# A planner's rule on VectorE and GpSimd: two-operand operations no longer exclude GpSimd

## The chip, the cores and the metric

The kernel runs on one core of a Trainium2 chip. Its engines work side by side, each through its own list of instructions in order: TensorE (PE in the profile; PEld is its weight load) multiplies, VectorE (DVE) and ScalarE (ACT) do elementwise work and reductions, GpSimd (POOL) does elementwise work on SBUF alone, and SyncE (SP) issues DMAs. The metric is device time in microseconds (us) for one execution, lower is better.

## The reference

Sliding-window attention with sink tokens, followed by a feed-forward network whose weights are float64 values drawn as float32; int64 and float64 inputs arrive as pairs of 32-bit words.

```python
# q, k, v: (4, 8, 768, 64) float32; n_sink = 4, window = 128
scores = matmul(q, k.transpose) / 8
keep   = (key < n_sink) | (0 <= query - key < window)
a      = exp(where(keep, scores, -1e9) - rowmax)
a      = a / (a.sum(-1) + 1e-9)
x      = matmul(a, v), heads merged        # (3072, 512)

h  = x @ w_in                              # (3072, 2048)
sp = log1p(exp(min(h, 20)))                # h itself above 20
y  = (h * tanh(sp)) @ w_out                # (3072, 512)
```

## The kernel before

The 3072 tokens are cut into 12 chunks of 256 (2 blocks of 128 queries). The four chunks that begin a batch come first, since their attention is smaller (plain fp32 products); the other eight follow. For each chunk there is attention in four pairs of heads (`pair`), then 8 steps of the feed-forward network (`step`), each over two 128-wide slices of the hidden dimension, `f`. The weights stay in SBUF. The first three chunks (`GROUP`) are taken in turn, two steps each (`PART`), so that the weights can be unpacked while they run; from chunk 3 on a chunk runs through its 8 steps alone, and all of these but the last chunk's have a form of their own (`wide`). Chunks are numbered from 0 in the order in which they run.

**Split values.** Products that need more precision than one fast pass are done in parts: a value m becomes a rounded copy gh and a rest gl = m - gh. So a rounded copy (`copy_ways`, lines 256 on ACT, 258 and 259 on VectorE) is followed nearly everywhere by a subtraction (`sub_ways`, line 267 on GpSimd, line 269 on VectorE). There are four kinds of subtraction: `gl<-n,gh` (hidden values, 96 of them, the last two given to VectorE alone), `w<-w,w` (32 rests of weights and 32 of Q), `w<-raw,w` (64 of K, on 64 partitions) and `w<-att,w` (48 rests of x, which read PSUM and are given to VectorE alone).

**Weights** (`weights`, 32 times): a DMA brings a 128x512 tile of float64 bit patterns (`raw`); s1 scales the high words (L297 on ACT, L298 on VectorE), s2 shifts (L300), s3 puts the sign in (L301), s4 masks the exponent (L303), s5 scales the low words (L305), s6 adds both (the join: L308 on GpSimd, L309 on VectorE), s7 copies and s8 subtracts.

**A step**: two groups of products into `hp` (L493 and L494 in wide steps, L497 in the others); in wide steps a reduction adds hp's two halves into n (L503). Then exp (L506, ACT), min (L507, VectorE), square, log, exp (L508, L509, L510, ACT), and one VectorE operation on u and h (L511), where h is n in SBUF for wide steps and hp in PSUM for the others. Then the copy to gh and the subtraction to gl, and the second products into `acc` (L527), those with gh first, those with gl behind.

**Attention of a pair**: Q K products (L396, or L399 from chunk 4 on), masked minimum (L407, VectorE, from PSUM), exp (L410, ACT), the normaliser (L413 or L414, L415), scaling by it (L420 on VectorE or L421 on ACT), transposes on PE (L431, L440), copies to SBUF, and the products with V (L449, L453).

**The plan.** All this is written as tasks with a rank, a few `ways` (engine, duration in ns, the call) and what they depend on. `Plan.solve` is a list scheduler that runs when the program is built: of all tasks that are ready it takes the one with the earliest start (plus the way's penalty, the fourth entry), and among equal starts the lowest rank. The order that comes out is kept on every engine, so on the chip each engine works through it however late things run. A scalar `port` stands for what VectorE and GpSimd share: a task on GpSimd, or one whose way has a fifth entry, starts only when `port` is free and holds it to its end. `shared()` makes such a way:

```python
def shared(way, pen=0):
    return way[0], way[1], 0, pen, True
...
ports = lambda t, e: e == POOL or len(t.ways[e]) > 4
...
key = (max(r, free[e]) + (t.ways[e][3] if len(t.ways[e]) > 3 else 0), rank[id(t)])
```

[...]

**Ranks.** `att_rank` places a pair's attention a number of steps ahead of the chunk that uses it: 20, 14 and 8 for the first three, and from chunk 3 on `min(LEAD, LEADN + (n - GROUP) / 2)`, with `LEADN` = 9. A pair's K, Q and V loads rank 3 steps (V 2) ahead of that; the splitting of K and Q follows 1.5 steps behind the loads. `OTP` places the transposes within the pair, and `OVP` the products with V.

Of the kernel before, what the change touches and what calls it, by code (L numbers as in the profile page):

```python
# [16 lines left out]
U32 = mybir.dt.uint32  # L17
AF = mybir.ActivationFunctionType
ALU = mybir.AluOpType
# [17 lines left out]
SIGN = -2147483648  # L37
# [3 lines left out]
PE, ACT, DVE, POOL, SP = "pe", "act", "dve", "pool", "sp"  # L41
# [1 line left out]
LAG = {PE: {PE: 0, ACT: 200, DVE: 200}, ACT: {PE: 270, ACT: 143, DVE: 142, POOL: 170}, DVE: {PE: 200, ACT: 120, DVE: 127, POOL: 155},  # L43
       POOL: {PE: 203, ACT: 75, DVE: 80, POOL: 102}, SP: {}}
W2 = 2 * P + SK
PEN_C, PEN_S, PEN_N, PEN_J = 200, 0, 0, 0
OTP, OVP = 1.2, 1
WA, WB, WO = 1.5, -5, 1.5
GROUP, PART = 3, 2
LEAD, LEADG, LEADN = 11, (20, 14, 8), 9  # L50
WARM, SPARE, ROOM = 14, 250, 4
ZERO = 224
SPL = 1.5
# [5 lines left out]
def f32(ap):  # L59
    return ap.bitcast(F32)  # L60


def act_t(n, psum=False, ptr=0):
    return (n + (61 if psum else 112)) / 1.2 + 93 * ptr


def dve_t(n, fast=False):
    return ((n / 2 if fast else n) + 66) / 0.96


def shared(way, pen=0):

    return way[0], way[1], 0, pen, True


def pool_t(n):
    return 149 + 2.1 * n


def pe_t(*ns):  # L80
# [25 lines left out]
class Plan:  # L106
# [6 lines left out]
    def add(self, prio, ways, deps=(), bufs=(), new=()):  # L113
        deps = {id(d): d for d in list(deps) + [b.maker for b in bufs] if d is not None}
        t = Task(prio, ways, list(deps.values()), list(bufs) + list(new), list(new))
        for b in t.bufs:
            b.users += 1
        for b in new:
            b.maker = t
        self.tasks.append(t)  # L120
        return t
# [108 lines left out]
class Fast(Base):  # L230
# [32 lines left out]
    def sub_ways(self, n, dst, a, b, engines=(POOL, DVE)):  # L263
        nc = self.nc
        ways = {}
        if POOL in engines:
            ways[POOL] = pool_t(n), lambda: nc.gpsimd.tensor_tensor(dst(), a(), b(), ALU.subtract)  # L267
        if DVE in engines:
            way = dve_t(n), lambda: nc.vector.tensor_tensor(dst(), a(), b(), ALU.subtract)  # L269
            ways[DVE] = shared(way, PEN_S) if POOL in engines else way  # L270
        return ways

    def load(self, prio, buf, dst, src, kb, **kw):
# [12 lines left out]
    def weights(self, f, rank):  # L286
        nc, add = self.nc, self.plan.add
        deps = []
        for src, nm in ((self.w_in, "wi"), (self.w_out, "wo")):
            raw = Buf("raw", [P, 512, 2], I32)  # L290
            z, e, hi, lo = Buf("w", [P, 512], I32), Buf("w", [P, 512], I32), Buf("w", [P, 512], F32R), Buf("w", [P, 512], F32R)
            hi.users, lo.users = 1, 1
            z.brief = e.brief = True
            r = rank if nm == "wi" else rank + WO
            ld = self.load(r - 1.0, raw, lambda raw=raw: raw.t.rearrange("p n t -> p (n t)"), src[f].bitcast(I32), 512)
            hw = lambda raw=raw: raw.t[:, :, 1]
            s1 = add(r, {ACT: (act_t(512), lambda z=z, hw=hw: nc.scalar.activation(f32(z.t), f32(hw()), AF.Copy, scale=2.0 ** -112)),  # L297
                         DVE: shared((dve_t(512), lambda z=z, hw=hw: nc.vector.tensor_scalar(f32(z.t), f32(hw()), 2.0 ** -112, None, ALU.mult)), PEN_C)},  # L298
                     [ld], [raw], [z])
            s2 = add(r + .01, {DVE: shared((dve_t(512, True), lambda z=z: nc.vector.tensor_scalar(z.t, z.t, 3, None, ALU.logical_shift_left)))}, [s1], [z])  # L300
            s3 = add(r + .02, {DVE: shared((dve_t(512), lambda z=z, hw=hw: nc.vector.scalar_tensor_tensor(  # L301
                z.t, hw(), SIGN, z.t, ALU.bitwise_and, ALU.bitwise_or)))}, [s2], [raw, z])
            s4 = add(r + .03, {DVE: shared((dve_t(512, True), lambda z=z, e=e: nc.vector.tensor_scalar(  # L303
                e.t, z.t, EXPM, None, ALU.bitwise_and)))}, [s3], [z], [e])
            s5 = add(r + .04, {DVE: shared((dve_t(512), lambda raw=raw, e=e: nc.vector.scalar_tensor_tensor(  # L305
                f32(e.t), raw.t[:, :, 0].bitcast(U32), 2.0 ** -52, f32(e.t), ALU.mult, ALU.mult)))}, [s4], [raw, e])
            s6 = add(r + .06, {
                POOL: (pool_t(512), lambda z=z, e=e: nc.gpsimd.tensor_tensor(f32(z.t), f32(z.t), f32(e.t), ALU.add)),  # L308
                DVE: shared((dve_t(512), lambda z=z, e=e: nc.vector.tensor_tensor(f32(z.t), f32(z.t), f32(e.t), ALU.add)), PEN_J)}, [s5, s3], [z, e])  # L309
            s7 = add(r + .07, self.copy_ways(512, lambda hi=hi: hi.t, lambda z=z: f32(z.t)), [s6], [z], [hi])  # L310
            s8 = add(r + .08, self.sub_ways(512, lambda lo=lo: lo.t, lambda z=z: f32(z.t), lambda hi=hi: f32(hi.t)), [s7], [z, hi], [lo])
            self.wh[nm].append(hi)
            self.wl[nm].append(lo)
            deps += [s7, s8]
        return deps
# [152 lines left out]
    def step(self, st, f2, rank, begins, ends, wdeps, last, wide):  # L468


        nc, add = self.nc, self.plan.add
# [4 lines left out]
        r = rank - (SH if last else 0)  # L476
        eager = last and f2 >= NF // 2 - QUICK
        u, m = Buf("u", [P, 2, T]), Buf("n", [P, 2, T])
# [26 lines left out]
        h = m if wide else hp  # L505
        a = add(r + .5, {ACT: (act_t(N, not wide), lambda: nc.scalar.activation(u.t, h.t, AF.Exp))}, hs or g1, [h], [u])  # L506
        a = add(r + .51, {DVE: shared((dve_t(N, True), lambda: nc.vector.tensor_scalar(u.t, u.t, E20, None, ALU.min)))}, [a], [u])  # L507
        a = add(r + .52, {ACT: (act_t(N, ptr=1), lambda: nc.scalar.activation(u.t, u.t, AF.Square, bias=self.one))}, [a], [u])  # L508
        a = add(r + .53, {ACT: (act_t(N, ptr=1), lambda: nc.scalar.activation(u.t, u.t, AF.Ln, bias=self.half, scale=0.5))}, [a], [u])  # L509
        a = add(r + .54, {ACT: (act_t(N), lambda: nc.scalar.activation(u.t, u.t, AF.Exp, scale=-1.0))}, [a], [u])  # L510
        way = dve_t(N), lambda: nc.vector.scalar_tensor_tensor(m.t, u.t, 1.0, h.t, ALU.subtract, ALU.mult)  # L511
        e = add(r + .55, {DVE: shared(way) if wide else way}, [a], [u, h], [] if wide else [m])
        gg = add(r + .57, self.copy_ways(N, lambda: gh.t, lambda: m.t), [e], [m], [gh])
        gk = add(r + .58, self.sub_ways(N, lambda: gl.t, lambda: m.t, lambda: f32(gh.t)), [gg], [m, gh], [gl])
        if eager:
# [2 lines left out]
        r = rank  # L518
# [380 lines left out]
```

## Time and profile before

| | |
|---|---|
| time, median of 2 runs | 735.19 us (734.97 to 735.41) |
| the profiled execution, its own time | 734.82 us |
| its span, first to last instruction | 732.8 us |
| granted TensorE clock, mean | 0.998 |
| GpSimd: subtractions and joins | 101, of 254 that may run there |
| `gl<-n,gh` on GpSimd / on VectorE | 32, mean 1293 ns / 64, mean 754 ns |
| `w<-w,w` (L267 / L269) | 24, mean 1387 ns / 40, mean 727 ns |
| `w<-raw,w` on GpSimd / on VectorE | 24, mean 1214 ns / 40, mean 658 ns |
| joins L308 / L309 | 21, mean 1403 ns / 11, mean 688 ns |

Busy time is the union of an engine's records, and its share is an average over the whole span, so it has to be read by stretches. A group's line reads: code line, engine, operation, what is written from what, shape and count, then busy us and the mean ns of one, then the engine's idle time ahead of it and what ended that. [...]

### The profile page before, as it was taken

The page shows a single profiled execution, that of the slowest core. Times are in us where ns is not written, and L with a number is a line of the kernel's source. Part 1 is how long each engine was busy: PE and PEld are TensorE (multiplying, and loading weights), DVE is VectorE, ACT ScalarE, POOL GpSimd, SP SyncE. Part 2 cuts the span into 40 slices and gives each one's busy share as a digit, 9 for nine tenths or more (in the row PEclk, how much of TensorE's full clock was granted, in tenths as well). Part 3 has the DMA queues.
Part 4 walks back from the last instruction along what each step waited for, and adds up shares of the span by engine and source line. Part 5 has one row for each costly group of instructions (what it writes and reads, how often), then busy time and mean ns, then how long its engine had stood idle before and what let it go on. Part 6 is the DMA issues. An engine that isn't in the chain of part 4 may idle for free.

```text
span 732.8 us, 12975 instructions
## 1 busy us (share of the span) xinstructions
PE 717.3 (98%) x4468; PEld 605.3 (83%) x4468; DVE 543.9 (74%) x1419; ACT 569.8 (78%) x1288; POOL 134.0 (18%) x109
## 2 busy tenths in 40 slices
PE   6999999999999999999999999999999999999996
PEld 4667889888888888888888888888888888888995
DVE  5999999996778877768877667777777867664432
ACT  5999989777977788787788878787787788775653
POOL 0232231201120222121012121130132223100000
PEclk9999999999999999999999999999999999999999
DMA  6555433423353323323233323223313311100000
GB/s 212 163 172 166 139 103 133 124 86 90 103 138 93 82 75 89 81 74 98 65 92 93 79 65 102 72 64 111 87 45 95 109 31 34 49 17 2 30 1 33
DMA packets 48987, 64.12 MB, mean 87 GB/s; under 512 B 4880, under 2 KB 41744, under 8 KB 48912
## 3 DMA queue, kind: packets, MB, share of 16 engines
q1 hardware_dynamic: 48480, 61.62, 29.0%
q10 hardware_dynamic: 432, 1.57, 0.6%
q8 instruction: 37, 0.61, 0.4%
q14 instruction: 38, 0.31, 0.1%
HBM read 56.89 MB, written 6.29 MB: 86 GB/s over the span
## 4 chain that ended last, share of the span: by engine, by line
PE 90%; DVE 4%; ACT 4%; DMA 1%; issue 1%; SPq 0%; ACTq 0%; DVEq 0%
PE acc L527 35%; PE hp L493 16%; PE hp L497 10%; PE hp L494 8%; PE att L449 5%; PE att L399 4%; PE att L431 4%; PE att L453 3%; PE att L497 2%; ACT p L410 1%; PE att L396 1%; DMA qh<-q_p 1%; ACT p L421 1%; DVE p L407 1%; ACT w L256 1%; DVE w L305 1%
## 5 line engine op out<-in xcount | busy, mean ns | idle before, releaser
L527 PE MATMUL acc<-w,gh 128*128 128x512 f32 x768 | 198.4, 396 | 0.2 <-ACT gh L256 0.2
L493 PE MATMUL hp<-w,w 128*128 128x512 f32 x512 | 192.1, 409 | 0.0
L527 PEld LDWEIGHTS acc<-w,gh 128*128 128x128 f32 x768 | 136.1, 188 | 26.3 <-ACT gh L256 0.8
L494 PE MATMUL hp<-w,w 128*128 128x256 f32 x512 | 143.3, 280 | 0.0
L503 DVE TENSOR_REDUCE n<-hp 128x256 f32<-128x512 f32 x128 | 87.8, 687 | 30.5 <-PE hp L494 29.6
L493 PEld LDWEIGHTS hp<-w,w 128*128 128x128 f32 x512 | 96.3, 188 | 17.1 <-issue 0.2
L527 PE MATMUL acc<-w,gl 128*128 128x512 f32 x384 | 108.3, 390 | 0.0
L410 ACT ACTIVATE p<-p,nm 128x288 f32<-128x288 f32 (+1 forms) x192 | 95.3, 499 | 3.6 <-DVE nm L407 3.5
L494 PEld LDWEIGHTS hp<-w,w 128*128 128x128 f32 x512 | 96.8, 189 | 1.5
L407 DVE CUSTOM_DVE_ANT_0 p<-att,m 128x288 f32<-128x288 f32 (+1 forms) x192 | 74.6, 419 | 25.2 <-PE att L399 20.2
L508 ACT ACTIVATE u<-u,bias 128x512 f32<-128x512 f32 x96 | 69.0, 720 | 29.8 <-DVE u L507 29.8
L497 PE MATMUL hp<-w,w 128*128 128x256 f32 x672 | 89.6, 285 | 0.2 <-DVE n L511 0.2
L497 PEld LDWEIGHTS hp<-w,w 128*128 128x128 f32 x672 | 84.9, 191 | 3.9 <-issue 0.5
L527 PEld LDWEIGHTS acc<-w,gl 128*128 128x128 f32 x384 | 71.9, 188 | 14.1
L506 ACT ACTIVATE u<-n 128x512 f32<-128x512 f32 x64 | 40.5, 632 | 54.1 <-DVE n L503 54.1
L267 POOL TENSOR_TENSOR gl<-n,gh 128x512 fp32r<-128x512 f32 x32 | 41.4, 1293 | 202.6 <-ACT gh L256 173.1
L256 ACT ACTIVATE gh<-n 128x512 fp32r<-128x512 f32 x93 | 58.3, 626 | 20.4 <-DVE n L511 20.3
L507 DVE TENSOR_SCALAR u<-u 128x512 f32<-128x512 f32 x96 | 44.7, 466 | 38.2 <-ACT u L506 37.6
L509 ACT ACTIVATE u<-u,bias 128x512 f32<-128x512 f32 x96 | 68.9, 718 | 1.7
L511 DVE SCALAR_TENSOR_TENSOR n<-u,n 128x512 f32<-128x512 f32 x64 | 44.1, 690 | 35.1 <-ACT u L510 34.9
L510 ACT ACTIVATE u<-u 128x512 f32<-128x512 f32 x96 | 60.1, 627 | 1.8
L269 DVE TENSOR_TENSOR gl<-n,gh 128x512 fp32r<-128x512 f32 x64 | 48.2, 754 | 15.4 <-PE acc L527 12.2
(85 smaller groups left out, 1063.3 us busy)
## 6 DMA issues: line engine op xcount, KB each, us to landing
raw<-k_p SPq DMA_DIRECT2D x64, 224.0 KB, 3.5
w<-q_p SPq DMA_DIRECT2D x64, 128.0 KB, 3.2
raw<-w_out SPq DMA_DIRECT2D x15, 512.0 KB, 4.0
raw<-w_in SPq DMA_DIRECT2D x14, 512.0 KB, 3.5
y<-u SPq DMA_DIRECT2D x24, 256.0 KB, 2.0
vt<-v_b SPq DMA_DIRECT2D x32, 192.0 KB, 2.5
vsr<-v_s SPq DMA_DIRECT2D x32, 128.0 KB, 2.3
ks<-k_p SPq DMA_DIRECT2D x16, 144.0 KB, 3.4
```

The costliest lines, as they stand in the source:

```text
L256: ways[ACT] = act_t(n, psum), lambda: nc.scalar.activation(dst(), src(), AF.Copy, scale=scale or 1.0)
L269: way = dve_t(n), lambda: nc.vector.tensor_tensor(dst(), a(), b(), ALU.subtract)
L407: a = add(r + .03 + .01 * e, {DVE: (dve_t(n) + 8, lambda st=st, pv=pv, nm=nm, e=e, mask=mask, n=n: nc.vector.tensor_tensor_reduce(out=pv() ...
L410: a = add(r + .05 + .01 * e, {ACT: (act_t(n, ptr=2), lambda pv=pv, nm=nm, sm=sm, e=e: nc.scalar.activation(pv(), pv(), AF.Exp, bias=nm.t[: ...
L493: yield nc.tensor.matmul(hp.t, wih[f].t[:, fs], xt, start=kt == 0, stop=False)
L494: yield nc.tensor.matmul(hp.t[:, 0, :], wil[f].t[:, fs], xt[:, 0, :], start=False, stop=kt == KT - 1)
L497: yield nc.tensor.matmul(hp.t[:, y, :], w_.t[:, fs], xt[:, z, :], start=kt == 0 and n_ == 0, stop=kt == KT - 1 and n_ == 2)
L503: hs.append(add(r + .3 + .1 * y, {DVE: (dve_t(2 * T), lambda y=y, hp=hp: nc.vector.tensor_reduce(m.t[:, y, :], hp.t.rearrange("p z t -> p ...
L508: a = add(r + .52, {ACT: (act_t(N, ptr=1), lambda: nc.scalar.activation(u.t, u.t, AF.Square, bias=self.one))}, [a], [u])
L509: a = add(r + .53, {ACT: (act_t(N, ptr=1), lambda: nc.scalar.activation(u.t, u.t, AF.Ln, bias=self.half, scale=0.5))}, [a], [u])
L510: a = add(r + .54, {ACT: (act_t(N), lambda: nc.scalar.activation(u.t, u.t, AF.Exp, scale=-1.0))}, [a], [u])
L527: yield nc.tensor.matmul(acc[t].t, g_.t[:, y, ts_], w_.t, start=new and n_ == 0, stop=done)
```

## The change

In the plan, `shared()` is taken off the VectorE ways that read two operands: the subtractions of `sub_ways`, s3, s5 and s6 of the weights, and L511 in wide steps. It also goes from s1 on VectorE, which reads one operand with a stride. The one-operand operations s2, s4, L507, L420 and the SBUF copies keep it. Penalties change: 150 ns on a subtraction on VectorE where GpSimd could take it (0 before), 250 on the join (0 before), 100 on copies on VectorE (200 before). GpSimd's duration in the plan goes from 149 + 2.1 n to 200 + 2.15 n ns. `OTP` goes from 1.2 to 1.0 and `LEAD` from 11 to 9. The instructions themselves, their operands and number stay; which of two engines does an operation, and the order on every engine, come from the plan.

```diff
-PEN_C, PEN_S, PEN_N, PEN_J = 200, 0, 0, 0
-OTP, OVP = 1.2, 1
+PEN_C, PEN_S, PEN_N, PEN_J = 100, 150, 0, 250
+OTP, OVP = 1.0, 1.0
...
-LEAD, LEADG, LEADN = 11, (20, 14, 8), 9
+LEAD, LEADG, LEADN = 9, (20, 14, 8), 9
...
 def pool_t(n):
-    return 149 + 2.1 * n
+    return 200 + 2.15 * n
...
     def sub_ways(self, n, dst, a, b, engines=(POOL, DVE)):
...
             way = dve_t(n), lambda: nc.vector.tensor_tensor(dst(), a(), b(), ALU.subtract)
-            ways[DVE] = shared(way, PEN_S) if POOL in engines else way
+            ways[DVE] = (*way, 0, PEN_S) if POOL in engines else way
...
             s1 = add(r, {ACT: (act_t(512), lambda z=z, hw=hw: nc.scalar.activation(f32(z.t), f32(hw()), AF.Copy, scale=2.0 ** -112)),
-                         DVE: shared((dve_t(512), lambda z=z, hw=hw: nc.vector.tensor_scalar(f32(z.t), f32(hw()), 2.0 ** -112, None, ALU.mult)), PEN_C)},
+                         DVE: (dve_t(512), lambda z=z, hw=hw: nc.vector.tensor_scalar(f32(z.t), f32(hw()), 2.0 ** -112, None, ALU.mult), 0, PEN_C)},
...
-            s3 = add(r + .02, {DVE: shared((dve_t(512), lambda z=z, hw=hw: nc.vector.scalar_tensor_tensor(
-                z.t, hw(), SIGN, z.t, ALU.bitwise_and, ALU.bitwise_or)))}, [s2], [raw, z])
+            s3 = add(r + .02, {DVE: (dve_t(512), lambda z=z, hw=hw: nc.vector.scalar_tensor_tensor(
+                z.t, hw(), SIGN, z.t, ALU.bitwise_and, ALU.bitwise_or))}, [s2], [raw, z])
...
-            s5 = add(r + .04, {DVE: shared((dve_t(512), lambda raw=raw, e=e: nc.vector.scalar_tensor_tensor(
-                f32(e.t), raw.t[:, :, 0].bitcast(U32), 2.0 ** -52, f32(e.t), ALU.mult, ALU.mult)))}, [s4], [raw, e])
+            s5 = add(r + .04, {DVE: (dve_t(512), lambda raw=raw, e=e: nc.vector.scalar_tensor_tensor(
+                f32(e.t), raw.t[:, :, 0].bitcast(U32), 2.0 ** -52, f32(e.t), ALU.mult, ALU.mult))}, [s4], [raw, e])
             s6 = add(r + .06, {
                 POOL: (pool_t(512), lambda z=z, e=e: nc.gpsimd.tensor_tensor(f32(z.t), f32(z.t), f32(e.t), ALU.add)),
-                DVE: shared((dve_t(512), lambda z=z, e=e: nc.vector.tensor_tensor(f32(z.t), f32(z.t), f32(e.t), ALU.add)), PEN_J)}, [s5, s3], [z, e])
+                DVE: (dve_t(512), lambda z=z, e=e: nc.vector.tensor_tensor(f32(z.t), f32(z.t), f32(e.t), ALU.add), 0, PEN_J)}, [s5, s3], [z, e])
...
         way = dve_t(N), lambda: nc.vector.scalar_tensor_tensor(m.t, u.t, 1.0, h.t, ALU.subtract, ALU.mult)
-        e = add(r + .55, {DVE: shared(way) if wide else way}, [a], [u, h], [] if wide else [m])
+        e = add(r + .55, {DVE: way}, [a], [u, h], [] if wide else [m])
```

## What was predicted

> **What bounds the kernel now.** I read the page from the top: its first row for busy shares, its slices for where they hold.
>
> ```profile
> span 732.8 us, 12975 instructions
> PE 717.3 (98%) x4468; PEld 605.3 (83%) x4468; DVE 543.9 (74%) x1419; ACT 569.8 (78%) x1288; POOL 134.0 (18%) x109
> PE   6999999999999999999999999999999999999996
> DVE  5999999996778877768877667777777867664432
> ```
>
> TensorE (PE) is busy in every slice but the first and last, but VectorE (DVE) is full too in the first quarter. So the kernel has two stages. Busy time by stretch (PE, PEld, DVE, ACT, POOL; then clock and DMA) says the same, and shows that the granted clock is full:
>
> ```profile
> 25.00:50.00 25.00, 23.45 (x181) 15.76 (x181) 24.65 (x98) 24.14 (x86) 8.21 (x6) 1.00 0.62 188
> 50.00:100.00 50.00, 49.42 (x345) 40.69 (x344) 48.80 (x133) 48.80 (x120) 12.02 (x9) 1.00 0.43 133
> 100.00:150.00 50.00, 50.00 (x324) 45.09 (x323) 49.61 (x105) 42.87 (x86) 11.47 (x8) 1.00 0.39 128
> 150.00:200.00 50.00, 50.00 (x330) 44.30 (x329) 38.73 (x84) 39.19 (x78) 6.09 (x5) 1.00 0.33 91
> 400.00:500.00 100.00, 100.00 (x604) 84.60 (x603) 71.28 (x181) 79.87 (x179) 21.21 (x17) 1.00 0.29 79
> ```
>
> PE's busy time includes filler: matmuls on zeros that the plan puts where it foresees idle time (line 622). The same view for that line alone (PE, PEld):
>
> ```profile
> 25.00:100.00 75.00, 9.22 (x68) 6.13 (x68) 1.00 0.49 152
> 100.00:733.00 633.00, 0.35 (x2) 0.20 (x2) 1.00 0.27 76
> ```
>
> Between 25 and 100 us PE stands idle for 1.55 + 0.58 us and multiplies zeros for 9.22: 11.3 us. That is all a better plan can win there; after 100 us only 0.35 us of filler is left and PE has no gap. VectorE and ScalarE set the pace up to 100 us, PE after it. The stretch ahead of 25 us has filler too, but it waits for first loads and holds few subtractions; I take nothing from it.
>
> **The change, part by part.** The first part lets the plan run VectorE's operations on two operands beside GpSimd (POOL). Whether the chip does so is seen where the two met by accident. Around 100 us the timeline shows (start, duration), VectorE first:
>
> ```profile
> 99.32 0.69 DVE L305 SCALAR_TENSOR_TENSOR w<-raw,w 128x512 f32<-128x512 uint32 x1
> 99.92 0.68 DVE L309 TENSOR_TENSOR w<-w,w 128x512 f32<-128x512 f32 x1
> 100.53 0.68 DVE L511 SCALAR_TENSOR_TENSOR n<-u,hp 128x512 f32<-128x512 f32 x1
> 101.91 1.68 DVE L269 TENSOR_TENSOR gl<-n,gh 128x512 fp32r<-128x512 f32 x1
> ...
> 100.09 1.68 POOL L308 TENSOR_TENSOR w<-w,w 128x512 f32<-128x512 f32 x1 [7.00 <-DVE w L305]
> 101.74 1.30 POOL L267 TENSOR_TENSOR w<-w,w 128x512 fp32r<-128x512 f32 x1
> ```
>
> The subtraction at 101.91 met a GpSimd subtraction already running until 103.04; it took 1.68 us and ended 0.55 after it. Its kind takes 0.69, so 0.99 was spent standing still. The other way round, GpSimd's addition at 100.09 began inside L309 and took 1.68 instead of 1.30. The exception is L511 at 100.53, inside that addition: 0.68, undisturbed. Its second operand, hp, lies in PSUM. So the exclusion holds for two operands in SBUF, which is what the old plan assumes. The new plan drops a true constraint. Also read off here: VectorE's records overlap by 0.08 (starts at 99.32, 99.92, 100.53), so such an operation costs its engine 0.605 us.
>
> [...]
>
> Stage one, 25 to 150 us. Groups of that window (count, busy, mean ns):
>
> ```profile
> L305 DVE SCALAR_TENSOR_TENSOR w<-raw,w 128x512 f32<-128x512 uint32 x26 | 18.0, 705 | 0.1
> L301 DVE SCALAR_TENSOR_TENSOR w<-raw,w 128x512 int32<-128x512 int32 x26 | 17.6, 686 | 0.0
> L269 DVE TENSOR_TENSOR w<-w,w 128x512 fp32r<-128x512 f32 x22 | 15.2, 699 | 0.1
> L269 DVE TENSOR_TENSOR gl<-n,gh 128x512 fp32r<-128x512 f32 x14 | 12.6, 896 | 0.0
> L309 DVE TENSOR_TENSOR w<-w,w 128x512 f32<-128x512 f32 x7 | 4.8, 687 | 0.0
> L300 DVE TENSOR_SCALAR w<-w 128x512 int32<-128x512 int32 x26 | 10.8, 421 | 0.0
> L303 DVE TENSOR_SCALAR w<-w 128x512 int32<-128x512 int32 x26 | 10.7, 422 | 0.0
> L507 DVE TENSOR_SCALAR u<-u 128x512 f32<-128x512 f32 x15 | 6.3, 422 | 0.0
> L420 DVE TENSOR_SCALAR p<-p,rc 128x128 f32<-128x128 f32 (+1 forms) x15 | 6.2, 417 | 0.1
> ...
> L308 POOL TENSOR_TENSOR w<-w,w 128x512 f32<-128x512 f32 x19 | 26.5, 1399 | 87.2 <-DVE w L305 79.9 <-DVE rc L415 7.4
> L267 POOL TENSOR_TENSOR w<-w,w 128x512 fp32r<-128x512 f32 x4 | 5.3, 1332 | 6.2 <-ACT w L256 6.1
> ```
>
> What must run one at a time: 95 operations on two SBUF operands (26 + 26 + 22 + 14 + 7) at 0.605 = 57.5 us; 82 on one operand at 0.42 less the overlap of 0.08 = 27.9; 23 of GpSimd's at 1.30 = 29.9. Sum 115 of 125 us: the shared resource is 92% full already.
>
> What can move is the 43 subtractions and additions still on VectorE (22 + 14 + 7). GpSimd holds 23 of 66; I read "most" as three quarters, 50, so 27 move (guess between 10 and 43). VectorE gets 27 x 0.605 = 16.3 us back, GpSimd takes 27 x 1.30 = 35.1. Demand on the shared resource becomes 115 + 18.8 = 134 us in 125: 9 us too many. With 10 moved it is 122 and fits; with all 43 it is 145, 20 too many. It is full at 14 moves (10 us over 0.695). So VectorE's relief can't be had: an operation of 0.605 leaves it, and the next one that needs the port stands behind 1.30 of GpSimd. How much of the 9 us is on PE's path? From 150 to 200 us VectorE is idle for 11.3 us and can take work that slips; against that, PE follows the order of a plan that does not know the delay. I take half: **+4.5**. Ends: -11.3 (all filler and gaps go) and +20.
>
> Cruise, 200 to 650 us. In 400 to 500 (counts as above):
>
> ```profile
> L511 DVE SCALAR_TENSOR_TENSOR n<-u,n 128x512 f32<-128x512 f32 x14 | 9.7, 690 | 3.4 <-ACT u L510 3.4
> L269 DVE TENSOR_TENSOR gl<-n,gh 128x512 fp32r<-128x512 f32 x10 | 7.2, 722 | 0.0
> L269 DVE TENSOR_TENSOR w<-raw,w 64x448 fp32r<-64x448 f32 x5 | 3.1, 623 | 0.2
> L269 DVE TENSOR_TENSOR w<-w,w 128x512 fp32r<-128x512 f32 x2 | 1.4, 686 | 0.0
> ```
>
> These are 17 subtractions on VectorE beside 17 on GpSimd (21.21 us in the stretch, above). Three quarters of 34 is 25 or 26, so 8.5 move and GpSimd is busy for 21.2 + 8.5 x 1.25 = 32 us in 100. VectorE has 29 us idle here, so its relief buys nothing: PE is the bound. What can hurt is L511, two SBUF operands, in the chain from hp to gh that feeds PE. In the old plan it was kept clear of GpSimd. Now one in three of the 14 meets a GpSimd operation and waits half of it: 4.5 waits of 0.63. What covers them is the time between the copy of gh (ACT) and the weight load that needs it:
>
> ```profile
> 397.87 0.62 ACT L256 ACTIVATE gh<-n 128x512 fp32r<-128x512 f32 x1
> 398.59 1.72 PEld L527 LDWEIGHTS acc<-w,gh 128*128 128x128 f32 x8
> ...
> 418.11 0.62 ACT L256 ACTIVATE gh<-n 128x512 fp32r<-128x512 f32 x1
> 421.07 1.68 PEld L527 LDWEIGHTS acc<-w,gh 128*128 128x128 f32 x8
> ```
>
> The cover is 0.10 us in one step and 2.34 in another. If half the steps are tight, 2.25 waits lose 0.4 each: 0.9 us in 100, times 4.5 = **+4**. Ends: 0 (all covered) and 4.5 x 0.63 x 4.5 = +13. After 650 us little is left to move.
>
> The penalties and GpSimd's dearer price (1301 ns for 512 columns in the plan, against the 1300 at 101.74) only steer which engine is picked; the moves above contain them. Copies freer to use VectorE: this concerns SBUF copies and PSUM copies, where ACT has 20 us idle in 100 and VectorE 29. Neither bounds the cruise: 0, and if VectorE were full as in stage one, a cast there costs 0.34 us of the full resource, ten of them 3.4 (in the upper end). Transposes 0.2 step earlier, and attention of chunks 4 to 11 led by 9 steps instead of 9.5 to 11: these change ranks, not work. The chain of waits gives the step:
>
> ```profile
> 398.88 2.76 PE acc L527 x12
> 458.04 2.79 PE acc L527 x12
> ```
>
> 59.2 us for a chunk of 8 steps, 7.4 us a step; so transposes move 1.5 us forward and the last five chunks' attention up to 14.8 us back, with its K, Q and V loads on SP's queue. The slowest of those lands in 3.5 us and is issued 1.5 steps, 11 us, ahead of its first use:
>
> ```profile
> raw<-k_p SPq DMA_DIRECT2D x64, 224.0 KB, 3.5
> ```
>
> Chunk 3 has a lead of 9 already and its stretch shows no filler. I take 0, ends -1.5 and +3.
>
> **Sum.** The profiled execution took 734.8 us in all (span 732.8); the median is 0.4 above it. 734.8 + 4.5 + 4 = 743.3, plus 0.4: **744 us**.
>
> **The rivals.** *Relief wins (faster).* In stage one VectorE is 98% busy; if a moved subtraction blocks it for less than the 0.605 us that it frees, filler shrinks. Place: 25 to 100 us; price: about 7 of the 11.3 us, 728. It decides when VectorE's next operations are mostly on PSUM (L407, L511 with hp), which a GpSimd operation did not slow. Against it: 85 of VectorE's 125 us there are port work. *Nothing comes of it, 735.* GpSimd still keeps clear of one-operand work, so the plan finds few openings and moves under 14, or the cover of up to 2.34 us swallows the waits. For it: the old plan's collisions above cost PE nothing visible. *The port runs over, on the path (slower).* Nearly all 43 move, two thirds of the 20 us land on PE, and the cruise loses 8: 734.8 + 13 + 8 = 756. For it: from 100 us on PE has no filler, so lost time isn't made up.
>
> **How the numbers follow.** A small loss (738 to 749.5) 0.50; relief 0.16; nothing 0.14; overrun 0.20. The predicted time is the likeliest case's. The range 731 to 757 leaves out most of relief (0.11) and the upper part of the overrun (0.08). Two per cent, about what a measurement tells from no change, is 14.7 us: faster than 720.5 would need more than all filler and gaps of stage one, 0.02; slower than 749.9 is the overrun, 0.20; the rest 0.78.
>
> **What would show it.** Right: GpSimd's count over 150 and its busy share near 35%; in 25 to 150 us L301, L305, L309 and L269 with means well over 690 ns; GpSimd's L267 at 1.4 and more; idle time or longer gaps on PE between 25 and 200 us; L511 on n in the cruise over 690. Wrong: those means unchanged while GpSimd is fuller (the exclusion isn't what the rows suggest); less filler and an earlier end of the third chunk (relief); GpSimd's count near 109 (nothing moved). A slower cruise with L511 unchanged would put the loss on the ranks instead.

## The result, and the profile after

The changed kernel takes 769.32 us (median of 2 runs, 768.82 to 769.81) against 735.19: a ratio of 1.0466 with a 95% interval of 1.0449 to 1.0484, so 34 us slower. The prediction was 744 with a range to 757: the sign was right, and the loss was four times as large. The profiled execution took 769.81 us, with this page:

```profile
span 768.0 us, 13016 instructions
PE 728.8 (95%) x4432; PEld 603.7 (79%) x4432; DVE 561.7 (73%) x1342; ACT 562.9 (73%) x1262; POOL 272.4 (35%) x212
PE   6898998788999999999999999999999999999997
DVE  5999989998678668677677677678678667865322
```

GpSimd's busy share is 35%, as forecast. VectorE's total went up (543.9 to 561.7 us) although it runs 77 instructions fewer: the first sign that its instructions became longer. TensorE has lost slices in the first quarter, which the stretches show in us (PE, PEld, DVE, ACT, POOL, then clock and DMA):

```profile
25.00:50.00 25.00, 21.53 (x155) 14.25 (x155) 24.88 (x91) 21.39 (x71) 10.99 (x8) 1.00 0.59 165
50.00:100.00 50.00, 44.08 (x277) 35.30 (x274) 46.55 (x107) 37.87 (x96) 27.86 (x20) 0.91 0.40 119
100.00:150.00 50.00, 44.05 (x271) 37.15 (x269) 47.92 (x85) 35.65 (x70) 26.43 (x18) 0.98 0.34 111
150.00:200.00 50.00, 43.87 (x266) 37.84 (x267) 42.51 (x64) 33.03 (x58) 26.27 (x19) 1.00 0.29 82
400.00:500.00 100.00, 98.68 (x585) 82.20 (x584) 72.12 (x174) 74.98 (x168) 33.46 (x26) 1.00 0.29 82
```

From 50 to 200 us TensorE now stands idle for 18 us (150 less 44.08, 44.05 and 43.87), where it had half a microsecond. VectorE is as busy from 25 to 200 us as before: the DVE column adds up to 161.9 us, and to 161.8 in the rows of before, with GpSimd at 92 us instead of 38. The work that left VectorE was replaced by standing still. The clock column is new too: 0.91 and 0.98, where the same stretches of before had 1.00.

How much of the 34 us belongs to which stage can be read from one line of each trace, the reductions that only the wide steps (chunks 3 to 10) have. Before, then after, in the view of the tile n; "209.7 to 679.0" are the starts of the first and the last of them:

```profile
L503 DVE TENSOR_REDUCE n<-hp x128: 670/686/693, 209.7 to 679.0; 128x256 f32<-128x512 f32 x128
```

```profile
L503 DVE TENSOR_REDUCE n<-hp x128: 669/683/693, 235.4 to 712.7; 128x256 f32<-128x512 f32 x128
```

The wide steps begin 25.7 us later (stage one, the first three chunks), last 8.0 us longer (the cruise), and the end adds 1.5. Groups from 25 to 150 us, after (count, busy, mean ns):

```profile
L301 DVE SCALAR_TENSOR_TENSOR w<-raw,w 128x512 int32<-128x512 int32 x22 | 22.5, 1028 | 0.1
L305 DVE SCALAR_TENSOR_TENSOR w<-raw,w 128x512 f32<-128x512 uint32 x21 | 16.9, 809 | 0.0
...
L303 DVE TENSOR_SCALAR w<-w 128x512 int32<-128x512 int32 x22 | 12.2, 562 | 0.0
...
L298 DVE TENSOR_SCALAR w<-raw 128x512 f32<-128x512 f32 x12 | 9.8, 822 | 0.0
L507 DVE TENSOR_SCALAR u<-u 128x512 f32<-128x512 f32 x12 | 7.8, 650 | 0.3 <-ACT u L506 0.2
L511 DVE SCALAR_TENSOR_TENSOR n<-u,hp 128x512 f32<-128x512 f32 x11 | 7.4, 677 | 0.1
L269 DVE TENSOR_TENSOR w<-w,w 128x512 fp32r<-128x512 f32 x6 | 7.2, 1208 | 2.3 <-ACT w L256 2.1
L414 DVE TENSOR_SCALAR rc<-sm 128x2 f32<-128x2 f32 x17 | 7.2, 424 | 0.8 <-ACT p L410 0.7
...
L308 POOL TENSOR_TENSOR w<-w,w 128x512 f32<-128x512 f32 x20 | 30.0, 1502 | 25.8 <-DVE w L305 20.0 <-DVE rc L414 3.3 <-ACT rc L413 2.5
L267 POOL TENSOR_TENSOR w<-w,w 128x512 fp32r<-128x512 f32 x16 | 22.4, 1405 | 30.5 <-ACT w L256 30.5
L267 POOL TENSOR_TENSOR gl<-n,gh 128x512 fp32r<-128x512 f32 x9 | 13.7, 1522 | 4.0 <-ACT gh L256 2.6 <-issue 1.3
```

L301 went from 686 to 1028 ns, L269 from 699 to 1208. One-operand work (L303, L507) is stretched as well: the plan still keeps it apart, but the order has slipped against the plan, so it meets GpSimd too. The same holds for s1 on VectorE (L298, 822 ns; the one of it before took 423), which the change also freed, and for the two-column L414, which neither plan keeps apart. L511 with its operand in PSUM is at 677, untouched. GpSimd's own operations take 1.41 to 1.52 us in the mean; in the same window before, its joins took 1.40 and its rests 1.33. One place in the timeline shows how the meetings chain (VectorE, then GpSimd):

```profile
158.68 0.68 DVE L305 SCALAR_TENSOR_TENSOR w<-raw,w 128x512 f32<-128x512 uint32 x1
159.28 1.78 DVE L301 SCALAR_TENSOR_TENSOR w<-raw,w 128x512 int32<-128x512 int32 x1
160.98 1.75 DVE L269 TENSOR_TENSOR gl<-n,gh 128x512 fp32r<-128x512 f32 x1
...
158.88 1.63 POOL L267 TENSOR_TENSOR w<-w,w 128x512 fp32r<-128x512 f32 x1 [0.75 <-ACT w L256]
160.47 1.71 POOL L308 TENSOR_TENSOR w<-w,w 128x512 f32<-128x512 f32 x1
```

GpSimd starts at 158.88 inside L305, is held (1.63), and then holds L301; its next operation starts at 160.47 inside L301, is held, and holds L269. The two take turns, and each 0.69 us of VectorE's work waits for 1.3 of GpSimd's. In the cruise the same is milder. First a group from 400 to 500 us, then TensorE's waits over the whole span (total us, times, longest):

```profile
L511 DVE SCALAR_TENSOR_TENSOR n<-u,n 128x512 f32<-128x512 f32 x14 | 10.5, 750 | 2.3 <-ACT u L510 1.9
```

```profile
PEld acc L527 <- ACT gh L256: 11.7, 18, 1.5
PE hp L497 <- DVE n L511: 7.5, 7, 2.0
PE acc L527 <- ACT gh L256: 7.0, 11, 1.3
```

Before, the weight loads behind gh waited 0.8 us in all, and L497 0.2. L497 is not part of the wide steps, so its waits belong to stage one; of the two waits for gh, 7.1 and 3.8 us fall between 235 and 713 us.

### The profile page after: what moved, and what is told of

The parts are those of the page before. It is cut to its first block, busy times and chain, and to the rows that moved or that the text cites. A ratio compares the mean times of both kernels' runs of the same rounds, so it can differ in the third digit from the quotient of the medians.

```text
span 768.0 us, 13016 instructions
## 1 busy us (share of the span) xinstructions
PE 728.8 (95%) x4432; PEld 603.7 (79%) x4432; DVE 561.7 (73%) x1342; ACT 562.9 (73%) x1262; POOL 272.4 (35%) x212
## 4 chain that ended last, share of the span: by engine, by line
PE 41%; DVE 29%; ACT 24%; issue 4%; DMA 1%; POOL 0%; ACTq 0%; SPq 0%; DVEq 0%; POOLq 0%
PE acc L527 17%; PE hp L493 7%; ACT p L410 4%; DVE n L511 4%; PE hp L494 4%; ACT p L421 3%; DVE w L269 3%; ACT gh L256 3%; PE hp L497 3%; ACT u L509 3%; DVE w L301 3%; ACT u L508 3%; ACT u L506 3%; ACT u L510 2%; PE att L449 2%
## 5 line engine op out<-in xcount | busy, mean ns | idle before, releaser
L267 POOL TENSOR_TENSOR gl<-n,gh 128x512 fp32r<-128x512 f32 x77 | 102.9, 1336 | 289.7 <-ACT gh L256 176.3
L493 PE MATMUL hp<-w,w 128*128 128x512 f32 x512 | 187.2, 404 | 0.0
L527 PE MATMUL acc<-w,gl 128*128 128x512 f32 x384 | 112.9, 395 | 1.8 <-DVE gl L269 1.8
L497 PE MATMUL hp<-w,w 128*128 128x256 f32 x672 | 91.2, 288 | 7.6 <-DVE n L511 7.5
L497 PEld LDWEIGHTS hp<-w,w 128*128 128x128 f32 x672 | 85.8, 192 | 13.9 <-DVE n L511 6.3
L421 ACT ACTIVATE p<-p,rc 128x288 f32<-128x288 f32 (+2 forms) x146 | 68.8, 503 | 34.2 <-DVE rc L415 33.8
L267 POOL TENSOR_TENSOR w<-raw,w 64x448 fp32r<-64x448 f32 x54 | 66.4, 1229 | 74.2 <-issue 23.6
L507 DVE TENSOR_SCALAR u<-u 128x512 f32<-128x512 f32 x96 | 47.4, 494 | 57.7 <-ACT u L506 57.6
L407 DVE CUSTOM_DVE_ANT_0 p<-att,m 128x288 f32<-128x288 f32 (+1 forms) x192 | 77.1, 417 | 15.2 <-PE att L399 11.1
L267 POOL TENSOR_TENSOR w<-w,w 128x512 fp32r<-128x512 f32 x43 | 57.9, 1348 | 61.0 <-ACT w L256 56.2
```

What stands on the lines that cost most here:

```text
L407: a = add(r + .03 + .01 * e, {DVE: (dve_t(n) + 8, lambda st=st, pv=pv, nm=nm, e=e, mask=mask, n=n: nc.vector.tensor_tensor_reduce(out=pv() ...
L421: ACT: (act_t(n, ptr=1), lambda row=row, rc=rc, e=e: nc.scalar.activation(row(), row(), AF.Copy, scale=rc.t[:, e:e + 1]), 0, PEN_N),
L493: yield nc.tensor.matmul(hp.t, wih[f].t[:, fs], xt, start=kt == 0, stop=False)
L497: yield nc.tensor.matmul(hp.t[:, y, :], w_.t[:, fs], xt[:, z, :], start=kt == 0 and n_ == 0, stop=kt == KT - 1 and n_ == 2)
L527: yield nc.tensor.matmul(acc[t].t, g_.t[:, y, ts_], w_.t, start=new and n_ == 0, stop=done)
```

## The experiments

Three theories stood at the start. A: the number of GpSimd operations that meet VectorE's unplanned makes the loss, so GpSimd's load counts. B: the plan's blindness alone makes a bad order. C: the ranks and the copies' penalty make it. Lines of the edited kernels are shifted by a few; operations are named as before.

**The exclusion alone taken out of the plan**, in the kernel before; the same edit in s1, s3, s5, s6 and L511.

```diff
-ways[DVE] = shared(way, PEN_S) if POOL in engines else way
+ways[DVE] = (*way, 0, PEN_S) if POOL in engines else way
...
```

> The kernel before with only the exclusion of two-operand operations taken out of the plan; penalties, ranks and GpSimd's price as before. GpSimd gets 106 operations (101 before, 204 in the changed kernel). Theory A (GpSimd's load times the plan's blindness: what costs is the number of GpSimd operations that meet two-operand VectorE work unplanned): about as much GpSimd work as before, so few more meetings: 738 to 748 us. Theory B (the plan's blindness alone makes the order bad): close to the changed kernel, 758 or more. Theory C (ranks, that is LEAD, OTP and the copies' penalty, make the loss): 735 plus or minus 2.

754.38 us, ratio 1.0253 (1.0224 to 1.0283). Theory A's number is missed by 6 us, B's by 4, C's by 17: with 106 operations on GpSimd for 101, blindness costs 19 us. Groups from 25 to 150 us show where:

```profile
L305 DVE SCALAR_TENSOR_TENSOR w<-raw,w 128x512 f32<-128x512 uint32 x24 | 22.5, 946 | 0.0
...
L309 DVE TENSOR_TENSOR w<-w,w 128x512 f32<-128x512 f32 x14 | 14.7, 1049 | 0.1
```

They had 705 and 687 ns before. Nearly all of the loss is in stage one: the first wide reduction starts at 228.2 us, and the wide steps last 470.0 (209.7 and 469.3 before).

```profile
L503 DVE TENSOR_REDUCE n<-hp x128: 664/684/694, 228.2 to 698.2; 128x256 f32<-128x512 f32 x128
```

How much GpSimd does counts less than whether the plan keeps it apart.

**Ranks and copies put back**, in the changed kernel.

```diff
-PEN_C, PEN_S, PEN_N, PEN_J = 100, 150, 0, 250
-OTP, OVP = 1.0, 1.0
+PEN_C, PEN_S, PEN_N, PEN_J = 200, 150, 0, 250
+OTP, OVP = 1.2, 1
...
-LEAD, LEADG, LEADN = 9, (20, 14, 8), 9
+LEAD, LEADG, LEADN = 11, (20, 14, 8), 9
```

> The changed kernel with OTP 1.2, LEAD 11 and the copies' penalty of 200 put back; exclusion still out, penalties on subtraction and join still in, 202 GpSimd operations. Theory A: the loss stays, 762 to 772 us. Theory B: the same. Theory C: it goes, 735 to 742.

760.95 us, a microsecond under what A and B had. Theory C falls as the main cause: these edits are worth 8.4 us of the 34. They aren't worth nothing, as the prediction had it.

**Penalties on subtraction and join, and GpSimd's price, put back**, in the changed kernel.

```diff
-PEN_C, PEN_S, PEN_N, PEN_J = 100, 150, 0, 250
+PEN_C, PEN_S, PEN_N, PEN_J = 100, 0, 0, 0
...
-    return 200 + 2.15 * n
+    return 149 + 2.1 * n
```

> The changed kernel with the penalties on subtraction and join back at 0 and GpSimd's old price; exclusion out, ranks new, 119 GpSimd operations. Theory A: most of the loss goes with the load, 738 to 750 us. Theory B: it stays, 758 or more. Theory C: it stays, 765 or more.

760.69 us: within B's expectation, and outside A's and C's. Taking GpSimd from 204 to 119 operations wins 8.6 us, not most of the loss. The first two runs split it in steps: 19.2 us for the exclusion (735.2 to 754.4), 6.6 more for penalties and price (to 761.0), 8.4 more for ranks and copies (to 769.3).

**A GpSimd that hardly reads**, in the changed kernel's order.

```diff
+def head(op, dst, a, b, fill):
+    part = lambda t, s: t[(slice(None),) * (len(t.shape) - 1) + (s,)]
+    op(part(dst, slice(0, 2)), part(a, slice(0, 2)), part(b, slice(0, 2)))
+    return fill(f32(part(dst, slice(2, None))), 0.0)
...
```

> The changed kernel in its own order, but each GpSimd operation does its first 2 columns only and fills the other 510 (or 446) with zeros, so that GpSimd writes for about as long but hardly reads SBUF. The rests and the joined weights are thus left out of the result. If meetings on the shared read side cost the time (theory A), two-operand VectorE operations no longer stretch (L301 and L269 w<-w,w back near 690 ns from 989 and 1120) and the time falls to 735 to 745 us; one-operand operations may still be held. If GpSimd's longer time in the chain (about 1.3 us for 0.69) or the order itself costs it (theories B, C), it stays at 760 or more. If writing alone excludes as much as reading, it stays too, with the stretched means.

729.24 us, ratio 0.9912 (0.9883 to 0.9940), 6 us under the expected range. With next to no reads the changed order is 40 us faster than with them, and faster than the kernel before. But GpSimd's operation also became shorter (about 0.7 us: 141.8 us for 204 of them and some set-up), so two controls followed.

**The same, held longer**: the zeros are written twice.

```diff
+    fill(f32(part(dst, slice(2, None))), 0.0)
     return fill(f32(part(dst, slice(2, None))), 0.0)
...
```

> As the run without reads (the rests and joined weights left out of the result, 2 columns computed), but with the zeros written twice, so that GpSimd is held nearly as long as in the changed kernel (about 1.1 to 1.2 us for 1.3). If reading is what excludes: two-operand means stay near 690 ns and the time is 729 to 737. If it was the shorter time on GpSimd that helped in that run: 745 or more. One-operand operations may be held longer.

730.22 us, ratio 0.9931 (0.9909 to 0.9954). GpSimd is busy for 246.8 us, near the changed kernel's 272.4, and the loss is still gone. Groups from 25 to 150 us (L312, L308, L310 and L514 are what L305, L301, L303 and L507 are above), and the first wide reduction:

```profile
L312 DVE SCALAR_TENSOR_TENSOR w<-raw,w 128x512 f32<-128x512 uint32 x28 | 19.0, 681 | 0.0
L308 DVE SCALAR_TENSOR_TENSOR w<-raw,w 128x512 int32<-128x512 int32 x26 | 17.7, 683 | 0.1
...
L310 DVE TENSOR_SCALAR w<-w 128x512 int32<-128x512 int32 x27 | 13.4, 507 | 0.0
...
L514 DVE TENSOR_SCALAR u<-u 128x512 f32<-128x512 f32 x16 | 8.5, 529 | 0.1
```

```profile
L510 DVE TENSOR_REDUCE n<-hp x128: 681/692/693, 204.7 to 673.7; 128x256 f32<-128x512 f32 x128
```

Two-operand work is at its undisturbed 681 to 683 ns beside a GpSimd that writes (and reads 2 to 4 columns of an operation); of the one-operand work s4 and L507 are still held (507 and 529 for 422), while s2 stays at 414 (421 before). In the changed kernel, beside GpSimd's full reads, the two-operand s3 had 1028 ns where it has 683 here.

**Half of the columns read.**

```diff
+    n = dst.shape[-1] // 2
+    op(part(dst, slice(0, n)), part(a, slice(0, n)), part(b, slice(0, n)))
+    return fill(f32(part(dst, slice(n, None))), 0.0)
...
```

> The changed kernel's order with the first half of the columns computed by GpSimd and the other half filled with zeros (that half of the rests and joined weights is left out of the result); about 1.0 us on GpSimd, of which 0.7 reads. If the loss follows the time for which GpSimd reads, about half of the 40 us between the run without reads (729) and the changed kernel (769) is left, perhaps less since short holds find more cover: 738 to 750. If reading at all is enough: 760 or more.

736.30 us, 2 us under the expected range. Half the reading brings 6 of the 39 us that lie between the run held longer and the changed kernel. The loss grows faster than the reading time; why is open.

**The blind plan without reads**: the kernel with the exclusion alone taken out, with `head` of the run held longer.

```diff
-ways[POOL] = pool_t(n), lambda: nc.gpsimd.tensor_tensor(dst(), a(), b(), ALU.subtract)
+ways[POOL] = pool_t(n), lambda: head(lambda d, x, y: nc.gpsimd.tensor_tensor(d, x, y, ALU.subtract), dst(), a(), b(), nc.gpsimd.memset)
...
```

> The kernel before with the exclusion out of the plan (754.4 us), each GpSimd operation again computing 2 columns and writing zeros twice over the rest (rests and joined weights left out of the result). If all of the 19 us come from VectorE and GpSimd meeting on reads, the time is 726 to 735, no more than before. If the blind plan's order is bad in itself: 740 or more.

734.64 us, ratio 0.9998 (0.9987 to 1.0010): the 19 us of the blind plan are gone. Its order isn't bad in itself, so theory B falls as it was put. Meetings on reads are the whole cost there; A was right in that, and wrong that the load sets it. The kernel before has a few meetings too and wasn't run without reads, so a worse order of a microsecond or two could hide behind them.

**s3 issued twice**, in the kernel before: VectorE time without GpSimd.

```diff
+            def sign(z=z, hw=hw):
+                for _ in range(2):
+                    yield nc.vector.scalar_tensor_tensor(z.t, hw(), SIGN, z.t, ALU.bitwise_and, ALU.bitwise_or)
...
```

> The kernel before with s3 of the weights (L301, 32 of them, all in the first 200 us) issued twice by VectorE without the plan knowing; the second gives the same bits. That is 32 x 0.605 = 19.4 us more of VectorE. If VectorE's time in stage one is paid nearly in full (so that standing still was the mis-sized term): 747 to 757 us. If half of it finds cover, as the prediction assumed for its term: 742 to 747. If the meetings' other effects made the loss: under 742.

757.20 us, ratio 1.0304 (1.0282 to 1.0326): 22.3 us more. A pair takes 1.41 us in the timeline, so the second s3 starts 0.72 us after the first and not the expected 0.605; 32 of them are 23 us of VectorE, and nearly all of it is paid. The doubled operation (over the whole span), one pair, and two stretches:

```profile
L303 DVE SCALAR_TENSOR_TENSOR w<-raw,w 128x512 int32<-128x512 int32 x64 | 43.7, 688 | 1.2
```

```profile
56.20 1.41 DVE L303 SCALAR_TENSOR_TENSOR w<-raw,w 128x512 int32<-128x512 int32 x2
```

```profile
50.00:100.00 50.00, 45.55 (x315) 36.36 (x316) 48.70 (x131) 44.08 (x115) 11.19 (x9) 1.00 0.43 131
100.00:150.00 50.00, 44.35 (x282) 38.40 (x280) 49.56 (x104) 39.43 (x80) 9.95 (x8) 1.00 0.31 106
```

TensorE loses about as much there (45.55 and 44.35 busy) as in the changed kernel, with GpSimd as idle as before. In stage one the old plan leaves next to no slack on VectorE: a microsecond there is a microsecond of the kernel.

**The exclusion back in the changed kernel's plan**, everything else new. What the expectation calls B' is what was left of B by then: unplanned meetings cost, whoever causes them.

```diff
-ways[DVE] = (*way, 0, PEN_S) if POOL in engines else way
+ways[DVE] = shared(way, PEN_S) if POOL in engines else way
...
```

> The changed kernel with the exclusion of two-operand operations put back in the plan and everything else new. Since VectorE's way now waits for the same free port and bears the penalty on top, the plan gives all 254 operations to GpSimd, and it foresees the waits (303 zero matmuls instead of 66). Theory B' (unplanned meetings cost, whoever causes them): few meetings, but 254 x 1.3 us on GpSimd, much of it in stage one, so a planned slow start: 745 to 765 us, with two-operand means near 690 ns. Theory A (GpSimd's load decides): more load than in the changed kernel, 770 or more.

771.62 us. The sighted plan with these penalties is as slow, for another reason: the ways of both engines wait for the same port and the planner compares starts, so a penalty of 150 on VectorE's way gives all 254 operations to GpSimd.

```profile
50.00:100.00 50.00, 48.48 (x341) 39.85 (x342) 40.44 (x108) 43.39 (x108) 29.34 (x22) 0.97 0.39 122
100.00:150.00 50.00, 46.13 (x310) 40.80 (x309) 38.07 (x71) 36.92 (x78) 31.21 (x25) 0.94 0.31 98
```

VectorE is no longer full (38.07 of 50), GpSimd is the fullest so far (31.21), and TensorE's busy time holds many of the 303 zero matmuls. At this end theory A's number (770 or more) comes out, and B' is 7 us too low: so many operations at 1.3 us cost time even when they are planned.

**Ranks and copies alone**, in the kernel before, with the exclusion known to the plan.

```diff
-PEN_C, PEN_S, PEN_N, PEN_J = 200, 0, 0, 0
-OTP, OVP = 1.2, 1
+PEN_C, PEN_S, PEN_N, PEN_J = 100, 0, 0, 0
+OTP, OVP = 1.0, 1.0
...
-LEAD, LEADG, LEADN = 11, (20, 14, 8), 9
+LEAD, LEADG, LEADN = 9, (20, 14, 8), 9
```

> The kernel before with only the ranks new: OTP 1.0, LEAD 9, copies' penalty 100; exclusion known to the plan, other penalties 0, old price; 128 GpSimd operations. In the blind plan these three edits cost about 7 to 8 us (769.3 against 761.0, and 760.7 against 754.4). If they hurt by themselves, they cost the same here: 741 to 744. If they only hurt through more meetings in the blind plan, they cost little: 733 to 738.

741.85 us, ratio 1.0091 (1.0062 to 1.0121): they cost by themselves. Then each edit alone.

```diff
-LEAD, LEADG, LEADN = 11, (20, 14, 8), 9
+LEAD, LEADG, LEADN = 9, (20, 14, 8), 9
```

> The kernel before with LEAD 9 for 11 alone. All three rank and copy edits together cost 6.7 us in this plan (741.85 against 735.15), from chunk 10 on. If the shorter lead is the cause, it costs 4 to 7 alone: 739 to 742. Otherwise 734 to 737.

734.26 us, ratio 0.9987 (0.9976 to 0.9997): alone, the lead costs nothing.

```diff
-PEN_C, PEN_S, PEN_N, PEN_J = 200, 0, 0, 0
+PEN_C, PEN_S, PEN_N, PEN_J = 100, 0, 0, 0
```

> The kernel before with the copies' penalty 100 for 200 alone. If freer copies on VectorE are the cause of the 6.7 us: 739 to 742. Otherwise 734 to 737. What neither this run nor the one with the lead shows is left to the transposes or to the three together.

737.67 us, ratio 1.0041 (1.0028 to 1.0054): 2.7 us.

```diff
-OTP, OVP = 1.2, 1
+OTP, OVP = 1.0, 1
```

> The kernel before with OTP 1.0 for 1.2 alone (80 GpSimd operations come out). If the transposes make the rest of the 6.7 us: 738 to 740. If it takes the edits together: 733 to 737.

739.13 us, ratio 1.0058 (1.0037 to 1.0080): 4.2 us. The three singles, -0.8, 2.7 and 4.2, add up to 6.1 of the 6.7, but their losses lie elsewhere, as the table in the next section shows: the copies and the transposes lose in stage one, the three together in the cruise. So the sum is no proof that the 6.7 is made of them. By which waits any of them costs stays open: each reshuffles the whole plan.

**More exclusion in the plan.** In the trace of before, the two-column operation L414, one operand and not excluded, is longer in the mean than the 0.17 us that it takes alone:

```profile
L414 DVE TENSOR_SCALAR rc<-sm 128x2 f32<-128x2 f32 x64 | 14.6, 228 | 8.8 <-ACT p L410 8.5
```

Two runs put it into the plan of the kernel before, with GpSimd's price as in the changed one; the second has LEAD 9 as well.

```diff
-DVE: (72, lambda rc=rc, sm=sm: nc.vector.tensor_scalar(rc.t, sm.t, 1e-9, None, ALU.add))}
+DVE: shared((72, lambda rc=rc, sm=sm: nc.vector.tensor_scalar(rc.t, sm.t, 1e-9, None, ALU.add)))}
...
-    return 149 + 2.1 * n
+    return 200 + 2.15 * n
```

> The kernel before with more of what the traces show put into its plan: the 2-column one-operand operation L414 also excludes GpSimd (it took 616 ns where it met GpSimd, 165 otherwise), and GpSimd's operation is priced at 200 + 2.15 n ns. 93 GpSimd operations. If meetings are what costs, fewer of them gain a little: 731 to 735 us. If the old plan's few meetings are covered, 734 to 737.

733.42 us, ratio 0.9979 (0.9969 to 0.9988): a little faster than the kernel before, and the fastest version here that computes everything. L414 is undisturbed:

```profile
L414 DVE TENSOR_SCALAR rc<-sm 128x2 f32<-128x2 f32 x57 | 9.5, 166 | 9.6 <-ACT p L410 9.2
```

> The kernel before with L414 excluded in the plan, GpSimd's higher price, and LEAD 9 (89 GpSimd operations). If the small gains of the two runs add (1.6 and 0.8): 731.5 to 733.5. If they don't: 733 to 736.

734.05 us, ratio 0.9986 (0.9976 to 0.9996): the small gains don't add.

## Why the prediction was right in direction and wrong in size

The traces split each run's time by stage: the start of the first wide reduction, the time from it to the last one (the cruise), the rest, and for how long TensorE is idle in the cruise, in us of the profiled execution.

| run | first wide reduction | cruise | rest | TensorE idle in the cruise |
|---|---|---|---|---|
| before | 209.7 | 469.3 | 53.8 | 0.0 |
| exclusion alone out of the plan | 228.2 | 470.0 | 53.8 | 0.7 |
| changed, ranks and copies put back | 232.6 | 472.3 | 53.8 | 0.9 |
| changed | 235.4 | 477.3 | 55.3 | 5.1 |
| changed, without reads, held longer | 204.7 | 469.0 | 55.2 | 0.0 |
| blind plan without reads | 210.6 | 469.3 | 53.9 | 0.0 |
| s3 twice | 232.5 | 469.2 | 53.8 | 0.1 |
| ranks and copies alone | 208.9 | 475.4 | 55.3 | 4.0 |
| lead alone | 209.1 | 467.8 | 56.3 | 0.2 |
| copies alone | 212.2 | 469.6 | 53.9 | 0.0 |
| transposes alone | 213.1 | 469.6 | 53.8 | 0.0 |

New ranks also move a little work across these borders: of attention's 1408 products, 372 start ahead of the first wide reduction before, and 364 in the changed kernel and with ranks and copies alone. At some 0.3 us each (before, L399's have a mean of 295 ns and L449's 322) that is 2 to 3 us.

- **The exclusion is real** (read from the collision at 101.91 us): right. The runs without reads show that it makes the whole loss of the blind plan, and that GpSimd's reading is what excludes a two-operand operation. Between 25 and 150 us L301 has a mean of 1028 ns beside operations that read all their columns, and 683 beside those that read 2 to 4 and write the rest.
- **Stage one, +4.5 us: the step that failed.** It measured 25.7, beyond its upper end of 20; with ranks and copies put back 22.9 of it is still there, and 18.5 with the exclusion alone out of the plan. The text reckoned by how much the shared resource overflows (9 us in 125), and took half, since VectorE has 11 idle microseconds after 150 us. But the stage runs at VectorE's pace in a fixed order, so what has to be priced is the time for which VectorE stands, whether the port overflows or not: s3 issued twice pays 22 us for 23, and the blind plan pays 19 us with only 5 more operations on GpSimd. And it stands for long. Added up over the operations of the first 250 us that GpSimd can hold, what each took beyond the undisturbed median of its kind is 52 us in the changed kernel and about 10 in the run held longer without reads; these two have the same order, and their wide steps start 30.7 us apart (235.4 and 204.7). So about three quarters of the standing was paid; some of the 30.7 may be the lower clock's (last section). Half of the 52 us is two-operand work. Some 16 are one-operand work that the plan still keeps apart, and 5 each are L414 and s1: once the order has slipped, planned exclusions fail too, which the prediction's sum had no term for.
- **The relief exists, and is small.** Without reads the wide steps begin at 204.7 instead of 209.7 us, where the blind plan without reads, with half as many operations on GpSimd, begins them at 210.6. So some 5 us are what a freer VectorE is worth in stage one, near the first rival's 7; the runs differ in ranks and copies too. That rival fell at its deciding point, whether a moved subtraction blocks VectorE for less than 0.605 us; in the collisions at 159 and 161 us it blocks for 1.1.
- **The cruise, +4 us**: measured 8.0, inside its ends of 0 and 13, but only a part is the step's cause. L511 rose from 690 to 750 ns in the mean, and TensorE waits for gh, as the step had it. With ranks and copies put back L511 is longer still (884 ns), and the cruise is only 3.0 us longer than before: that is what the meetings cost, near the forecast's 4. With ranks and copies alone L511 is undisturbed (693 ns) and the cruise is 6.1 us longer, which is the sign that the forecast named for a loss by the ranks. So 5 of the 8 us came in with ranks and copies, and the sum landed inside the range partly by luck. L511 from 400 to 500 us, ranks and copies put back, then alone:

```profile
L511 DVE SCALAR_TENSOR_TENSOR n<-u,n 128x512 f32<-128x512 f32 x13 | 11.5, 884 | 5.5 <-ACT u L510 5.5
```

```profile
L511 DVE SCALAR_TENSOR_TENSOR n<-u,n 128x512 f32<-128x512 f32 x13 | 9.0, 693 | 6.1 <-ACT u L510 5.7
```

- **Ranks and copies, 0 with ends of -1.5 and +3: mis-sized.** They cost 6.7 us in the sighted plan and 8.4 in the changed one. In the sighted plan the loss lies in the cruise, where TensorE is idle for 4.0 us; no single edit makes it idle there (0.0 to 0.2), so it takes a combination of them, and which one stays open. In the changed order without reads the same ranks leave no idle time there (0.0 for 5.1), so this loss too needs a GpSimd that reads. That they change ranks and not work was no argument: the ranks decide the order, and the order decides which operations meet.
- **The overrun rival (756)** was the nearest, and still 13 us too low, since its price came from the same overflow.
- **GpSimd's count**, over 150 in the forecast, is 204. The penalties do what they are meant to do.

## What to carry to other kernels

A planner that doesn't know of an exclusion loses more than the overflow of the shared resource: it loses unplanned waits on the engine that sets the pace, here three quarters of them or more. So find first which engine has no slack in a stage, and price such a wait there nearly in full. Rules and penalties of a planner belong together: with the right rule back, the new penalties were as slow as without it, while the same new order was 5 us faster than the old kernel on a GpSimd that hardly reads.

## What the runs showed of the hardware

- Where VectorE with two operands in SBUF met a GpSimd operation that reads, in the timelines at 100 us before and at 159 us in the changed kernel, they excluded each other either way round: the first to start ran on, and the other's record was stretched, L301 to 1.78 us from 0.69 (at 159.28), a join on GpSimd to 1.71 from 1.30 (at 160.47). With one operand in PSUM VectorE wasn't touched: L511 on hp took 672 to 690 ns in all 28 records of the changed kernel, and 676 to 690 before. Beside GpSimd operations that read 2 to 4 columns and write the rest, two operands weren't touched (means of 681 and 683 ns), and the one-operand s4 and L507 were held (507 and 529 for 422).
- The operation on two columns, L414, was held for as long as a large one: among the changed kernel's 82 of them it has a mean of 386 ns and takes up to 1.23 us, 1.06 more than alone (L301 above: 1.09), and it has a mean of 166 where the plan keeps it apart.
- Idle time that the plan didn't foresee has no zero matmuls in it (66 were placed, 102 before), and in the changed kernel the granted clock was 0.91 between 50 and 100 us and 0.98 between 100 and 150. Against full clock that is 5.5 us by estimate (50 x 0.09 + 50 x 0.02); how much of it is in the 34 us was not measured by itself. That the idle time brought the clock down was not shown: with s3 twice TensorE is idle for about as long in these two stretches (4.45 and 5.65 us, for 5.92 and 5.95), at 1.00, and with the exclusion back in the plan, with 303 zero matmuls and less idle time (1.52 and 3.87), the clock is 0.97 and 0.94.
